# Sliding-window attention plus gated GLU on one Trainium2 core: the later chunks' normalised rows transposed through a DRAM scratch and VectorE, and a mask tile filled on another engine

## The chip, the cores and the metric

The kernel runs on 1 core of one Trainium2 chip. The metric is the device time of one execution in microseconds (us), the median of the runs of a kernel.

## The reference, cut to what matters

```python
xn = layernorm(x)                                  # x: 1 x 2048 x 640, no scale, no bias
qkv = xn @ wqkv                                    # 32 heads of 20
scores = q @ k.T * 20**-0.5                        # query i sees keys i-255 .. i
o = softmax(where(mask, scores, -1e9)) @ v
A = o @ wo
h = sigmoid(xn @ w_gate) * (xn @ w_up)             # 640 -> 1536
B = h @ w_down
out = x + A + B
```

All tensors are bf16. Every product of the normalised rows needs them with the 640 features on the partitions, because TensorE contracts over partitions. So the normalised x, whose rows have tokens on partitions, has to be transposed once. How this is done for three quarters of the tokens is what changes.

## The kernel before, in words

The 2048 tokens are cut into four chunks of 512 (`NCH`, `CW`), numbered 0 to 3. A chunk has four blocks of 128 tokens, called s = 0 to 3 (`SBC`), and the features make five blocks of 128, d = 0 to 4 (`DC`). For each chunk there are these stages:

- **norms.** `load_x` (L137) brings the chunk's rows to the tile `xc`, which has one buffer. `ln_block` (L261) takes means and variances on VectorE, one block at a time (two bn_stats at L252 and an aggregate at L258). `rstd_blocks` (L264) makes 1/sqrt(var+eps) on GpSimd. `norm_block` (L270, the operation is L272) writes the normalised rows to a tile `xn`. Then `xnT[c]`, the transposed chunk, is filled: for chunk 0 by TensorE (`transpose_rows`, L276), for chunks 1 to 3 by four DMA transposes from SP's queue (`turn_block`, L282, L283).
- **qk** (`g_qk`, L366): ten groups of five matmuls (L297) on `xnT`, copied out by VectorE (q, L301) or ScalarE (k, L303), stored to a DRAM scratch (L305) and loaded again spread by head (`spread`, L307, the DMA is L315).
- **v** (`g_v`, L385): eight groups of five matmuls (L326), copied out half by VectorE and half by ScalarE (both L335).
- **gu** (`g_gu`, L402): twelve pairs of a gate group (L411) and an up group (L418). ScalarE takes tanh of the gate (L414) and VectorE multiplies (`h`, L422).
- **scores, exp, mask, pv** (`scores`, L480; `pv`, L508): a step puts score matmuls (L487) into one PSUM tile, ScalarE takes the exponential into `pT` (L493), and GpSimd zeroes what the mask excludes (L504). In the last step of each group of a later chunk, VectorE does this instead with a minimum against the tile `edge` (L497). `pv` multiplies by v (L520). VectorE then transposes and scales the result (L532 to L548) into `oc`.
- **out** (`g_out`, L457): down projection (L432), output projection (L439), residual (`rows`, L443) and the store (L454).

TensorE's PSUM tiles of all stages but the scores come from one pool of four buffers, `ps_d`. A group of matmuls can start only when the reader of the tile that had its buffer is done.

The order of work on each engine is fixed by the program. The loop over score steps (L719) calls `fill.pull`, which takes pieces from a list of generators (L689 to L707), about 1800 ns of matmuls a step. `mix(a, b, first, every, rest)` (L595) runs generator `a` and, from its piece number `first` on, puts one step of `b` behind every `every`-th piece. So the norms of chunk 1 are threaded through the gu pieces of chunk 0, those of chunk 2 through `out0`, those of chunk 3 through `gu1b` and `out1`. Each engine then executes its own list in order: an instruction that waits holds up all that stands behind it on that engine, and SP's queue issues its DMAs in order as well.

`edge` (L236) is filled by GpSimd: a memset (L239) and four affine selects (L243). `make_edge` is called at L675, but GpSimd waits for nothing there and runs these instructions as soon as it reaches them.

Of the kernel before, what the change touches and what calls it, by code (L numbers as in the profile page):

```python
# [9 lines left out]
P = 128  # L10
S = 2048
D = 640
# [3 lines left out]
DC = D // P  # L16
FC = F // P
CW = 512
NCH = S // CW
SBC = CW // P  # L20
# [11 lines left out]
MULT = mybir.AluOpType.mult  # L32
SUB = mybir.AluOpType.subtract
# [3 lines left out]
BIG = 3.0e38  # L37
BF16 = mybir.dt.bfloat16
# [55 lines left out]
def kernel(  # L94
# [11 lines left out]
    nc = tc.nc  # L106
    x2 = A_x.flatten_outer_dims()
# [3 lines left out]
    def pool(name, bufs, **kw):  # L111
        return ctx.enter_context(tc.tile_pool(name=name, bufs=bufs, **kw))
# [3 lines left out]
    lnp = pool("lnp", 4)  # L116
# [18 lines left out]
    xc = {}  # L135

    def load_x(c):  # L137
        t = xp.tile([P, SBC, D], BF16, name="xc")
        xc[c] = t
        nc.sync.dma_start(out=t, in_=xr[:, c * SBC:(c + 1) * SBC, :])  # L140
# [39 lines left out]
    def load_gu(t, w, k, lo=0, hi=FS):  # L180
        nc.sync.dma_start(out=t[k][:, :, lo:hi],
                          in_=w.rearrange("(c p) f -> p c f", p=P)[:, :, k * FS + lo:k * FS + hi])
# [32 lines left out]
    def load_wo():  # L215
        for i in range(HG):
            nc.sync.dma_start(out=wo[32 * i:32 * i + 32, :, :],
                              in_=wo_i[i].rearrange("(m j) n -> j m n", j=32))
# [17 lines left out]
    edge = const.tile([P, HG, 2 * U], BF16, name="edge")  # L236

    def make_edge():
        nc.gpsimd.memset(edge, BIG)  # L239
        for k, base, sign in ((0, -1, -1), (1, 0, 1)):  # L240
            for a in range(2):
                view = edge[a * U:(a + 1) * U, :, k * U:(k + 1) * U]
                nc.gpsimd.affine_select(out=view, in_=view, pattern=[[0, HG], [sign, U]],  # L243
                                        compare_op=GE, fill=0.0, base=base, channel_multiplier=-sign)

    xnT = {}
    xns = {}
# [13 lines left out]
    def ln_block(c, s, mv=None):  # L261
        return ln_mv(ln_half(c, s, 1, ln_half(c, s, 0)), mv)

    def rstd_blocks(mvs):  # L264
        rstds = lnp.tile([P, SBC], FP32, name="rstds", bufs=1)
        nc.gpsimd.tensor_scalar(out=rstds, in0=mvs[:, :, 1], scalar1=EPS, scalar2=None, op0=ADD)
        nc.gpsimd.tensor_tensor(out=rstds, in0=rstds, in1=neghalf, op=POW)
        return rstds

    def norm_block(c, s, mv, rstd):  # L270
        xn = lnp.tile([P, D], BF16, name="xn")
        nc.vector.tensor_scalar(out=xn, in0=xc[c][:, s, :], scalar1=mv[:, 0:1],  # L272
                                scalar2=rstd[:, 0:1], op0=SUB, op1=MULT)
        xns[c, s] = xn
# [4 lines left out]
            nc.tensor.transpose(pt[:, d, :], xns[0, s][:, d * P:(d + 1) * P], ident)  # L279
        copy(out=xnT[0][:, lo:hi, s * P:(s + 1) * P], in_=pt[:, lo:hi, :])  # L280

    def turn_block(c, s):  # L282
        nc.sync.dma_start(out=xnT[c][:, :, s * P:(s + 1) * P], in_=xns.pop((c, s)), transpose=True)  # L283

    def new_xnT(c):
        xnT[c] = xtp.tile([P, DC, CW], BF16, name="xnT")
# [51 lines left out]
    def proj_v(c, s, hf, copy):  # L338
        copy_v(c, s, hf, project_v(c, s, hf), copy)

    MM = 216

    def g_norms(c, turn, gap=3):


        new_xnT(c)
        mvs = lnp.tile([P, SBC, nc.vector.BN_AGGR_DIM], FP32, name="mvs", bufs=1)
        for s in range(SBC):
            ln_block(c, s, mvs[:, s, :])
            if s == SBC - 1:  # L350
                rstds = rstd_blocks(mvs)
            yield 0
        for _ in range(gap):
            yield 0
        for s in range(SBC):
            norm_block(c, s, mvs[:, s, :], rstds[:, s:s + 1])
            yield 0
            if turn:
                turn_block(c, s)

    def g_turns(c):
        for s in range(SBC):
            turn_block(c, s)
            yield 0

    def g_qk(c):  # L366
        for w in "qk":
            for m in range(DC):
                proj_block(w, c, m)
                if c == 0 and w == "q" and m == 1:  # L370
                    load_x(1)
                if c == 0 and w == "q" and m == 3:
                    load_gu(wu, B_w_up, 0, FS // 2)
                if c == 1 and w == "q" and m == 3:
                    load_wo()
                if c and w == "k" and m == DC - 1:
                    spread("q", c, 0, GH)
                yield 5 * MM
        if c == 0:
            spread("q", c, 0, 2)  # L380
            spread("k", c, 0, 2)
            spread("q", c, 2, 4)
            spread("k", c, 2, 4)

    def g_v(c):  # L385
        for s in range(SBC):
            new_v(c, s)
            for hf in range(2):
                proj_v(c, s, hf, nc.scalar.copy if hf else nc.vector.tensor_copy)
                if hf == 0:  # L390
                    yield 5 * 136
            if s == 0:
                spread("k", c, 0, 2)
                spread("k", c, 2, GH)
            if s == 1:
                spread("q", c, GH, NG)
                spread("k", c, GH, NG)
            yield 5 * 136
# [4 lines left out]
    def part(w, d, f):  # L403
        k, first = divmod(f * P, FS)
        return w[k][:, d, first:first + P]

    def g_gu(c, f0, f1):
        for f in range(f0, f1):
            pg = ps_d.tile([P, CW], FP32, name="pg", tag="d")
            for d in range(DC):  # L410
                nc.tensor.matmul(pg, lhsT=part(wg, d, f), rhs=xnT[c][:, d, :],  # L411
                                 start=(d == 0), stop=(d == DC - 1))
            th = tp.tile([P, CW], FP32, name="th")
            nc.scalar.activation(out=th, in_=pg, func=TANH, scale=0.5)  # L414
            yield 5 * MM
            pu = ps_d.tile([P, CW], FP32, name="pu", tag="d")
            for d in range(DC):
                nc.tensor.matmul(pu, lhsT=part(wu, d, f), rhs=xnT[c][:, d, :],  # L418
                                 start=(d == 0), stop=(d == DC - 1))
            h = hp.tile([P, CW], BF16, name="h")  # L420
            ht[c, f] = h
            nc.vector.scalar_tensor_tensor(out=h, in0=th, scalar=1.0, in1=pu, op0=ADD, op1=MULT)  # L422
            yield 5 * MM
# [39 lines left out]
    def g_out(c, between, ahead=()):  # L463
        nxt = new_rows(c, 0)
        for s in range(SBC):
            rows = nxt
            if s == 0:
                yield from ahead
            if s + 1 < SBC:
                nxt = new_rows(c, s + 1)  # L470
            ys = [ps_d.tile([P, CW], FP32, name=f"y{i}", tag="d") for i in range(2)]
            for y, cut in zip(ys, HALVES):
                yield from down(c, s, y, cut)
            if s == 0:
                yield from between
            outp(c, s, ys, rows)
            yield 10 * 136
# [117 lines left out]
    def mix(a, b, first, every=1, rest=True):  # L595

        for k, cost in enumerate(a):
            yield cost
            if k >= first and (k - first) % every == 0:
                yield next(b, 0)  # L600
        if rest:
            yield from b
# [66 lines left out]
    nc.scalar.activation(out=scr, in_=neghalf[:, 0:1], func=EXP)  # L669
    banks.close()  # L670
    ps_s = banks.enter_context(tc.tile_pool(name="ps_s", bufs=1, space=bass.MemoryType.PSUM))
    for _ in g_qk(0):
        pass
    load_rest()
    make_edge()  # L675

    fill = Fill()
    GU = 10 * MM
    OUT = 4 * 34 * 136
    APART = 1800  # L680
    FIRST_PART = 1000
    def later(load, *args):
        load(*args)
        yield 0

    norms1 = g_norms(1, True)
    norms2 = g_norms(2, True)
    norms3 = g_norms(3, False, 6)
    fill.add("gu0a", mix(g_gu(0, 0, 4), norms1, 4, 1, False), 4 * GU)  # L689
    fill.add("gu0b", mix(g_gu(0, 4, 12), norms1, 0), 8 * GU)  # L690
    fill.add("x2", later(load_x, 2), 0)
    fill.add("wo_i", later(turn_wo), 0)
    fill.add("wd", later(load_wd), 0)
    fill.add("pads", later(clear_next), 0)
    fill.add("qk1", g_qk(1), 50 * MM)
    fill.add("v1", mix(g_v(1), g_gu(1, 0, 2), 1, 2), 40 * 136 + 2 * GU)
    fill.add("out0", mix(g_out(0, g_gu(1, 2, 3)), norms2, 1, 1), OUT + GU)
    fill.add("x3", later(load_x, 3), 0)
    fill.add("qk2", g_qk(2), 50 * MM)
    fill.add("v2", mix(g_v(2), g_gu(1, 3, 7), 0, 1), 40 * 136 + 4 * GU)  # L700
    fill.add("gu1b", mix(g_gu(1, 7, 12), norms3, 0, 1, False), 5 * GU)
    fill.add("out1", mix(g_out(1, g_gu(2, 0, 1)), itertools.chain(norms3, g_turns(3)), 1, 2), OUT + GU)
    fill.add("qk3", g_qk(3), 50 * MM)
    fill.add("v3", mix(g_v(3), g_gu(2, 1, 5), 0, 1), 40 * 136 + 4 * GU)
    fill.add("gu2", g_gu(2, 5, 12), 7 * GU)
# [38 lines left out]
    c = NCH - 1  # L744
# [6 lines left out]
    rows = [new_rows(c, s, *home, queue=nc.scalar) for s, home in enumerate(homes)]  # L751
# [55 lines left out]
```

## Time and profile before

| | before |
|---|---|
| runs, us | 309.04, 309.19, 309.59 (median 309.19) |
| span of the profiled execution, first to last instruction, us | 307.5 |
| TensorE busy (matmuls) | 299.6 us, 97% |
| VectorE, ScalarE, GpSimd busy | 170.7, 198.4, 169.3 us |
| DMA transposes | 12, from SP's queue |
| granted TensorE clock | 1.00 |

The profile's page gives the profiled execution by its span alone, which is 1.7 us below the median of the runs; what lies before the first and after the last instruction makes up the rest. A busy share is taken over the whole span. The lines below give times in us from the start of the span; "idle before" in square brackets is the time in which the engine stood still ahead of that piece, with what ended it.

### The profile page before, as it was taken

How to read it: one execution, taken by the hardware profiler on the slowest of the kernel's cores; microseconds unless marked ns; L12 is line 12 of the kernel's file. 1: busy time of each engine (PE TensorE's matmuls, PEld its weight loads, DVE VectorE, ACT ScalarE, POOL GpSimd, SP SyncE). 2: the span in 40 equal slices, each digit the busy share in tenths (PEclk: the TensorE clock that was granted, in tenths of full speed). 3: DMA queues.
4: the chain of work that ended last, by engine and by line, in shares of the span. 5: the costliest groups of instructions: out<-in, count | busy, mean ns of one | idle time of the engine just before them, and what ended most of it. 6: DMA issues, size and time to landing. Idle time of an engine off the chain costs nothing.

```text
span 307.5 us, 9944 instructions
## 1 busy us (share of the span) xinstructions
PE 299.6 (97%) x4276; PEld 167.5 (54%) x4311; DVE 170.7 (56%) x339; ACT 198.4 (65%) x197; POOL 169.3 (55%) x308
## 2 busy tenths in 40 slices
PE   7999999999999999999999999999999999999995
PEld 3654444555657654554457654554546664444774
DVE  5633666639698364487946164392824536363523
ACT  6933877698855649888674547878585547687000
POOL 6000686787874828576683729467372937566000
PEclk9999999999999999999999999999999999999999
DMA  7997976986407352820002712730000200000202
GB/s 215 366 344 236 324 158 214 337 238 209 154 2 139 58 179 68 272 83 2 3 3 67 129 58 87 250 122 0 5 0 2 87 26 21 2 2 7 83 21 67
DMA packets 40460, 35.68 MB, mean 116 GB/s; under 512 B 10560, under 2 KB 39872, under 8 KB 40384
## 3 DMA queue, kind: packets, MB, share of 16 engines
q1 hardware_dynamic: 39552, 34.27, 37.3%
q10 hardware_dynamic: 864, 0.77, 0.9%
q8 instruction: 34, 0.56, 0.8%
q14 instruction: 10, 0.08, 0.1%
HBM read 23.63 MB, written 10.26 MB: 110 GB/s over the span
## 4 chain that ended last, share of the span: by engine, by line
PE 96%; issue 1%; DMA 1%; DVE 1%; ACT 0%; SPq 0%
PE y L432 18%; PE pu L418 17%; PE pg L411 17%; PE pqk L297 14%; PE ps L487 9%; PE pv L326 7%; PE y L439 7%; PE acc L520 6%; DMA xc<-in_A_x_dram 1%; PE pt L279 0%; ACT xn L617 0%; DVE xn L272 0%; DVE xn L628 0%; SPq L156 0%; DVE stats L252 0%
## 5 line engine op out<-in xcount | busy, mean ns | idle before, releaser
L504 POOL TENSOR_SCALAR_AFFINE_SELECT pT<-pT 64x512 bf16<-64x512 bf16 (+1 forms) x256 | 157.7, 616 | 108.1 <-ACT pT L493 95.6
L493 ACT ACTIVATE pT<-ps 128x2048 bf16<-128x2048 f32 (+1 forms) x76 | 141.0, 1855 | 59.6 <-PE ps L487 54.6
L422 DVE SCALAR_TENSOR_TENSOR h<-th,pu 128x512 bf16<-128x512 f32 x48 | 32.8, 684 | 52.6 <-PE pu L418 46.1
L418 PE MATMUL pu<-xnT,wu 128*128 128x512 bf16 x228 | 59.0, 380 | 0.7 <-issue 0.2
L411 PE MATMUL pg<-xnT,wg 128*128 128x512 bf16 x226 | 58.5, 380 | 0.9 <-issue 0.3
L432 PE MATMUL y<-wd,h 128*128 128x320 bf16 (+2 forms) x396 | 56.7, 295 | 0.0
L432 PEld LDWEIGHTS <-h 128*128 128x128 bf16 x396 | 36.7, 98 | 15.8 <-issue 2.0
L414 ACT ACTIVATE th<-pg 128x512 f32<-128x512 f32 x48 | 28.6, 595 | 15.5 <-PE pg L411 15.4
L411 PEld LDWEIGHTS <-wg 128*128 128x128 bf16 x240 | 22.2, 98 | 25.8 <-issue 1.8
L418 PEld LDWEIGHTS <-wu 128*128 128x128 bf16 x240 | 22.0, 98 | 25.5 <-issue 2.0
L487 PE MATMUL ps<-qT,kT 20*64 20x320 bf16 (+4 forms) x1440 | 32.1, 260 | 0.0
L532 DVE STREAM_TRANSPOSE t<-acc 128x512 f32<-128x512 f32 x32 | 21.1, 697 | 19.7 <-PE acc L520 19.7
L487 PEld LDWEIGHTS <-kT 20*64 20x64 bf16 x1440 | 15.4, 103 | 24.9 <-issue 21.8
L443 DVE SCALAR_TENSOR_TENSOR rows<-y,rows 128x320 bf16<-128x320 f32 x30 | 14.4, 488 | 25.5 <-PE y L439 25.3
L544 DVE TENSOR_TENSOR on<-t,rec 128x320 bf16<-128x320 f32 (+4 forms) x48 | 27.8, 580 | 1.1
L326 PE MATMUL pv<-wv,xnT 128*128 128x320 bf16 x160 | 25.7, 300 | 0.0
L439 PE MATMUL y<-wo,oc 128*128 128x320 bf16 (+2 forms) x165 | 24.2, 295 | 0.0
L297 PE MATMUL pqk<-xnT,wk 128*128 128x512 bf16 x97 | 23.1, 381 | 0.2
L297 PE MATMUL pqk<-xnT,wq 128*128 128x512 bf16 x94 | 22.8, 381 | 0.4 <-issue 0.2
L335 DVE CAST v<-pv 64x320 bf16<-64x320 f32 x29 | 14.1, 486 | 12.5 <-PE pv L326 12.3
L520 PE MATMUL acc<-pT,v 64*32 64x320 bf16 (+4 forms) x1440 | 19.7, 253 | 0.0
L520 PEld LDWEIGHTS <-v 64*32 64x32 bf16 x1440 | 16.2, 91 | 5.8 <-ACT pT L493 1.7
(50 smaller groups left out, 178.7 us busy)
## 6 DMA issues: line engine op xcount, KB each, us to landing
qT<-sq SPq DMA_DIRECT2D x16, 256.0 KB
kT<-sk SPq DMA_DIRECT2D x16, 256.0 KB
sq<-st SPq DMA_DIRECT2D x20, 128.0 KB
sk<-st SPq DMA_DIRECT2D x20, 128.0 KB
out_dram<-rows SPq DMA_DIRECT2D x15, 160.0 KB
wg<-in_B_w_gate_dram SPq DMA_DIRECT2D x4, 480.0 KB
wu<-in_B_w_up_dram SPq DMA_DIRECT2D x4, 480.0 KB
xc<-in_A_x_dram SPq DMA_DIRECT2D x3, 640.0 KB
```

Source lines behind the costliest of these rows:

```text
L297: nc.tensor.matmul(ps, lhsT=wt[:, m, :], rhs=xnT[c][:, d, :], start=(d == 0), stop=(d == DC - 1))
L326: nc.tensor.matmul(ps[:, 0:HALF], lhsT=xnT[c][:, d, s * P:(s + 1) * P], rhs=wqkv[2][:, d, hf * HALF:(hf + 1) * HALF], start=(d == 0), stop ...
L411: nc.tensor.matmul(pg, lhsT=part(wg, d, f), rhs=xnT[c][:, d, :], start=(d == 0), stop=(d == DC - 1))
L414: nc.scalar.activation(out=th, in_=pg, func=TANH, scale=0.5)
L418: nc.tensor.matmul(pu, lhsT=part(wu, d, f), rhs=xnT[c][:, d, :], start=(d == 0), stop=(d == DC - 1))
L422: nc.vector.scalar_tensor_tensor(out=h, in0=th, scalar=1.0, in1=pu, op0=ADD, op1=MULT)
L432: nc.tensor.matmul(y[:, 0:cut[1] - cut[0]], lhsT=ht[c, f][:, s * P:(s + 1) * P], rhs=wd[:, f, cut[0]:cut[1]], start=(f == 0), stop=False)
L439: nc.tensor.matmul(y[:, 0:cut[1] - cut[0]], lhsT=oc[c, m][:, s * P:(s + 1) * P], rhs=wo[:, m, cut[0]:cut[1]], start=False, stop=(m == DC - 1))
L487: nc.tensor.matmul(ps[a * U:(a + 1) * U, i, col * U:(col + n) * U], lhsT=qk["k", kc, o // GH][32 * i:32 * i + DH, o % GH + a, kb * U:(kb + ...
L493: nc.scalar.activation(out=pt[:, :, 0:width], in_=ps[:, :, 0:width], func=EXP, scale=SCALE)
L504: nc.gpsimd.affine_select(out=view, in_=view, pattern=[[0, HG], [0, n], [sign, U]], compare_op=GE, fill=0.0, base=base, channel_multiplier ...
L520: nc.tensor.matmul(acc[32 * i:32 * i + 32, q * U:(q + n) * U], lhsT=vt[kb][a * U:(a + 1) * U, u, h * VW:h * VW + 32], rhs=pt[a * U:(a + 1) ...
```

## The change

For chunks 1 to 3 the DMA transposes go away. The normalised rows are written by VectorE with their features regrouped, stored by four DMAs of 160 KB to a scratch in DRAM (`xs`), and loaded back by four DMAs of 160 KB into the chunk's own `xc` tile, in runs of 320 bytes, so that partition 32b+j holds every 32nd token and the b-th quarter of the features. Five VectorE transposes of 32x32 blocks (`turn`), one for each d, then make `xnT[c]`. The steps of the norms generators are placed anew: `norms2` begins in `v1` and goes on in `out0`, the loads of x for chunks 2 and 3 move behind the first k store of the chunk before, and `lag` steps lie between the loads back and the first `turn`. Besides, `make_edge` moves ahead of the first qk stage and its memset goes to VectorE, while the selects stay on GpSimd.

```diff
-        nc.gpsimd.memset(edge, BIG)
+        nc.vector.memset(edge, BIG)
...
-    def turn_block(c, s):
-        nc.sync.dma_start(out=xnT[c][:, :, s * P:(s + 1) * P], in_=xns.pop((c, s)), transpose=True)
+    xs = [tc.dram_tile([CW, D], BF16, name=f"xs{k}") for k in range(2)]
+
+    def norm_grouped(c, s, mv, rstd):
+        xn = lnp.tile([P, D], BF16, name="xn")
+        nc.vector.tensor_scalar(out=xn.rearrange("p (b d i) -> p d b i", b=4, i=32),
+                                in0=xc[c][:, s, :].rearrange("p (d b i) -> p d b i", b=4, i=32),
+                                scalar1=mv[:, 0:1], scalar2=rstd[:, 0:1], op0=SUB, op1=MULT)
+        nc.sync.dma_start(out=xs[c % 2][s * P:(s + 1) * P, :], in_=xn)
+
+    def regroup(c):
+        rows = xs[c % 2].rearrange("(t j) (b f) -> b j t f", j=32, b=4)
+        for b in range(4):
+            nc.sync.dma_start(out=xc[c][32 * b:32 * b + 32].rearrange("j s (a f) -> j (s a) f", a=4), in_=rows[b])
+
+    def turn(c, d):
+        nc.vector.transpose(out=xnT[c][:, d, :].rearrange("p (t j) -> p t j", j=32),
+                            in_=xc[c].rearrange("p s (a f) -> p (s a) f", a=4)[:, :, 32 * d:32 * d + 32])
...
-    def g_norms(c, turn, gap=3):
-        new_xnT(c)
+    def g_norms(c, gap=3, lag=3):
...
         for s in range(SBC):
-            norm_block(c, s, mvs[:, s, :], rstds[:, s:s + 1])
+            norm_grouped(c, s, mvs[:, s, :], rstds[:, s:s + 1])
             yield 0
-            if turn:
-                turn_block(c, s)
-
-    def g_turns(c):
-        for s in range(SBC):
-            turn_block(c, s)
+        regroup(c)
+        for _ in range(lag):
+            yield 0
+        new_xnT(c)
+        for d in range(DC):
+            turn(c, d)
             yield 0
...
+                if c and w == "k" and m == 0 and c + 1 < NCH:
+                    load_x(c + 1)
...
+    make_edge()
     for _ in g_qk(0):
         pass
     load_rest()
-    make_edge()
...
-    norms1 = g_norms(1, True)
-    norms2 = g_norms(2, True)
-    norms3 = g_norms(3, False, 6)
-    fill.add("gu0a", mix(g_gu(0, 0, 4), norms1, 4, 1, False), 4 * GU)
+    norms1 = g_norms(1, 3, 7)
+    norms2 = g_norms(2)
+    norms3 = g_norms(3, 4, 4)
+    fill.add("gu0a", mix(g_gu(0, 0, 4), norms1, 1, 1, False), 4 * GU)
     fill.add("gu0b", mix(g_gu(0, 4, 12), norms1, 0), 8 * GU)
-    fill.add("x2", later(load_x, 2), 0)
...
-    fill.add("v1", mix(g_v(1), g_gu(1, 0, 2), 1, 2), 40 * 136 + 2 * GU)
+    fill.add("v1", mix(mix(g_v(1), g_gu(1, 0, 2), 1, 2), norms2, 3, 1, False), 40 * 136 + 2 * GU)
     fill.add("out0", mix(g_out(0, g_gu(1, 2, 3)), norms2, 1, 1), OUT + GU)
-    fill.add("x3", later(load_x, 3), 0)
...
-    fill.add("out1", mix(g_out(1, g_gu(2, 0, 1)), itertools.chain(norms3, g_turns(3)), 1, 2), OUT + GU)
+    fill.add("out1", mix(g_out(1, g_gu(2, 0, 1)), norms3, 1, 2), OUT + GU)
```

## The prediction

> **What bounds the kernel now.** I read the page's slices first (TensorE at 9 in 38 of 40), then TensorE's own waits, then the timelines of TensorE and VectorE around the places where the change works. TensorE's waits, in full but for the first row (columns: total us, times, longest):
>
> ```profile
> PE pt L279 <- DVE xn L272: 0.7, 1, 0.7
> PE pt L279 <- DVE xn L628: 0.5, 1, 0.5
> PE pg L411 <- issue: 0.3, 2, 0.2
> PE pqk L297 <- issue: 0.2, 1, 0.2
> PE pu L418 <- issue: 0.2, 1, 0.2
> ```
>
> After chunk 0's norms TensorE waits for nothing that has a name: matmuls follow each other from 13 us to 303 us. So there is little to win (at most the 1.2 us of the first two rows), and every new wait of TensorE is lost time. In particular no transpose of `xnT` by DMA is waited for: by the landing counts in the trace they land at 46.7, 102.7 and about 175.3 us, and qk starts at 54.6, 107.3 and 178.3 us.
>
> **The start.** GpSimd's selects of `edge` ran from 3.9 to 5.7 us. VectorE's norm at 4.81 us, beside them, took 0.64 us, the later ones at 7.61 and 9.60 us 0.45 us each. The change takes the selects away: at most 0.2 us, and the next transposes hang on ScalarE's root, which ends at 5.72 us either way. I take -0.1 (0 to -0.2). The memset on VectorE (0.69 us on GpSimd) fits into its 0.66 us pause before 14.18 us, and may cost 0.1 there.
>
> **Chunk 1.** The rows store behind the third norm at about 39.6 us, land at 43 (behind q and k transfers that land until 41.5), and the loads back, issued from 43 to 45, land near 47.6. The first `turn` stands behind the tenth `h`, at 51.1 us: that wait is covered by 3.5 us. The last turn stands behind the twelfth `h`:
>
> ```profile
> 53.06 1.24 PE L418 MATMUL pu<-xnT,wu 128*128 128x512 bf16 x5
> 54.59 2.35 PE L297 MATMUL pqk<-xnT,wq 128*128 128x512 bf16 x10
> ...
> 51.79 0.69 DVE L422 SCALAR_TENSOR_TENSOR h<-th,pu 128x512 bf16<-128x512 f32 x1 [0.59 <-PE pu L418]
> 54.57 0.69 DVE L422 SCALAR_TENSOR_TENSOR h<-th,pu 128x512 bf16<-128x512 f32 x1 [2.09 <-ACT th L414]
> ```
>
> A turn is not in the trace. Its nearest row is the transpose of `oc` (128x512 bf16, 0.71 us, next instruction 0.64 us after its start); I take that, although the turn reads in pieces of 64 bytes, and keep 0.4 to 1.0 us. The last h starts at 54.57 (ScalarE's tanh holds it), the fifth turn ends at about 55.95, and the fifth matmul of qk is due at 54.6 + 4 x 0.213 = 55.5: **+0.45** (0 to 1.9, the latter with turns of 1.0 us).
>
> **Chunk 2, in v of chunk 1.** Here the statistics, 4.0 us of VectorE (the eight bn_stats and four aggregates that ran from 86.81 to 90.79), move forward between the copies of v:
>
> ```profile
> 74.35 0.99 DVE L335 CAST v<-pv 64x320 bf16<-64x320 f32 x2
> 75.37 0.69 DVE L422 SCALAR_TENSOR_TENSOR h<-th,pu 128x512 bf16<-128x512 f32 x1
> 76.31 0.99 DVE L335 CAST v<-pv 64x320 bf16<-64x320 f32 x2 [0.25 <-PE pv L326]
> 79.21 0.99 DVE L335 CAST v<-pv 64x320 bf16<-64x320 f32 x2 [1.91 <-PE pv L326]
> 81.04 0.69 DVE L422 SCALAR_TENSOR_TENSOR h<-th,pu 128x512 bf16<-128x512 f32 x1 [0.83 <-PE pu L418]
> 81.92 1.31 DVE L532 STREAM_TRANSPOSE t<-acc 128x512 f32<-128x512 f32 x2 [0.19 <-PE acc L520]
> ```
>
> On the clock of before, counted from the end of the first row (75.3): two blocks of statistics to 77.3, h to 77.9, a third to 78.9, the third copy to 79.75, the fourth block to 80.75, the last copy to 81.7 instead of 80.2. By the changed program's waits, the second accumulator of the next `pv` takes the buffer that this last copy frees; it is due at about 80.95. So TensorE waits **+0.8** (0 to 1.5; pauses of 3 us shown above take up most of the 4). The x rows must have landed by 75.3; issued near 66, behind transfers that then land 4 us late, they do by about 71.5. They also lie ahead of four k stores. Scores need those k at 77.96, before they landed at 76.2; what is moved forward costs their 1.8 us of packets, but the same transfer no longer lies ahead at 45: I take nothing, 0 to 1.
>
> **Chunk 2, the round trip.** From 81.7 on VectorE has no pause: the first norm waits for GpSimd's roots (1.3 us behind the last statistics, 82.35), then norm, h, two transposes of acc, norm, the chain of scaling (3.7 us, as from 83.16 to 86.88 before), and two norms: 0.55 each, as in the rows of 0.41 to 0.75 us of the norms before. The last norm ends at about **90.15**. Only then can its store be issued. A store of 160 KB issued at 92.26 landed at 94.03, so this one lands at 91.95. The four loads wait for all four stores; a load of 160 KB took 2.3 us from issue to landing, three more issues follow at 0.45 us or three more transfers at 0.75 us: the last lands at about **96.5**. But VectorE comes to the first turn at 91.75, behind the residual of out0's first block. It stands still for 4.7 us, and behind the turns stands this:
>
> ```profile
> 91.35 0.88 DVE L443 SCALAR_TENSOR_TENSOR rows<-y,rows 128x320 bf16<-128x320 f32 x2
> 94.21 0.43 DVE L497 TENSOR_TENSOR pT<-pT,edge 128x512 bf16<-128x512 bf16 x1 [0.27 <-ACT pT L493]
> 95.06 0.87 DVE L443 SCALAR_TENSOR_TENSOR rows<-y,rows 128x320 bf16<-128x320 f32 x2
> ...
> 95.17 1.29 PE L520 MATMUL acc<-pT,v 64*32 64x320 bf16 x96
> 96.39 0.43 PE L487 MATMUL ps<-qT,kT 20*64 20x320 bf16 x24
> 96.75 2.62 PE L432 MATMUL y<-wd,h 128*128 128x320 bf16 x18
> ```
>
> Four turns bring it to 99.05, the minimum (0.43) to 99.5. The `pv` of before 95.17, shifted by the 0.8 to 95.97, needs the minimum's result two thirds through, at 96.75: it waits 2.8 us. After it, the down projection (96.75 in the last row) needs the buffer of the residual that follows the fifth turn: another 0.25. Together **+3.05**. Bounds: 1.0 (norms of 0.41, all loads in parallel, landing at 94.6) and 5.5 (norms of 0.75, turns of 1.0, transfers of 1.2 us each).
>
> **Chunk 3.** Its round trip has 8 us, from about 161 to the first turn at 169. The last turn stands behind the last residual of out1 (178.07 + 0.49), ends near 179.2, and the fifth matmul of qk is due at 179.2: **+0.1** (0 to 0.6). Where TensorE is late, ScalarE and GpSimd only gain slack, and SP's queue is left by 12 DMA transposes of 1.2 us issue each for 24 issues of 0.45.
>
> **The sum:** -0.1 + 0.45 + 0.8 + 3.05 + 0.1 = +4.3 us, on the span of 307.5: 311.8. The 1.7 us outside the span stay, so 309.19 becomes 313.5.
>
> **The rivals.** *Hidden round trip:* the rows are there when VectorE comes to chunk 2's first turn, and it never stands still. Price: the 3.05 go, and the total is 310.4; 309.6 if pauses absorb v's wait too, 309.2 without chunk 1's term, and 308.1 if the start's whole 1.2 us are won besides. It decides at one point: the last norm would have to end by about 85.4 instead of 90.15. For it speaks that my VectorE clock adds 25 durations in a row; against it that the list of VectorE puts two norms behind the scaling chain, which needs a `pv` that ends at 81.9. Chance 0.14.
>
> *Slow short runs:* the loads back write 2048 runs of 320 bytes. Packets of 384 bytes took 22 ns in the trace, of 640 bytes 32, of 1024 bytes 46: a line through these gives 20 ns, 2.6 us for all on 16 engines, which is inside the forecast. If a run under some length cost double, 2.6 us are added ahead of chunk 2's turns: 316.1; chunk 1 still has 3.5 of cover. The 256-byte packets of the DMA transposes at 18 ns speak against it. Chance 0.10. The Trainium skill, in "DMA: Bandwidth & Descriptors", section Specifications, puts the least run for full rate at 512 bytes, with a read-modify-write below; by that rule the time would be this rival's, and no row here shows a plain load of such runs.
>
> *Other causes,* mostly slower (a k transfer late for 77.96, turns that hold GpSimd): 0.06.
>
> The Trainium skill, in "VectorE: DVE Perf Modes", section The three transpose paths, calls VectorE's transpose the quickest for 32x32 blocks, 311 ns against 1309 ns by DMA for 128x128. It says nothing about the time, as the DMA's transposes held up nobody here.
>
> **How the numbers follow.** The forecast has 0.70, its own range 311.0 to 316.2 (each term's low or high end, not all at once). To hold 8 in 10 the range reaches down to 310.2 and up to 317.0, which takes in the slow runs and the upper part of the hidden case. About 0.2% (0.6 us) is what can be told from no change. Of the hidden case I count 0.07 as faster, 0.05 as the same and 0.02 as slower, of the other causes 0.01 each as faster and the same: 0.08, 0.06 and, with the rest, 0.86 slower.
>
> **What would show it.** Right: VectorE's waits list a new row, the turn waiting for a DMA of `xc` from `xs`, 4 to 5 us once, near 92 to 97 us; TensorE waits for the minimum (L512 after) about 2.8 us near 97, for VectorE's copy of v some 0.8 us near 81, and under a microsecond before qk of chunk 1. Wrong: TensorE's waits stay as above, or the stall sits in front of a qk stage or of chunk 1's first scores.

## The result, and the profile after

| | before | after |
|---|---|---|
| runs, us | median 309.12 (308.95 to 309.59, 4 runs) | median 317.63 (315.91 to 320.22, 4 runs) |
| ratio after to before | | 1.0281, 95% interval 1.0233 to 1.0329 |
| profiled execution, us | span 307.5 | 317.51, span 315.1 |
| TensorE, VectorE busy, us | 299.6, 170.7 | 305.6, 178.5 |

The prediction said 313.5 (310.2 to 317.0). The direction holds; the loss is about twice as large. The line numbers of the kernel after: norm L286, store to the scratch L289, loads back L295, turn L298, qk L313, pv of the v stage L342, v copy L351, h L437, down L447, output projection L454, residual L458, exp L508, minimum L512, `acc` L535, `t` L547, `oc` L563.

In the page's slices of the kernel after, the row of the granted TensorE clock is no longer 9 all along, as it was before:

```profile
PE   7999999999895999999999999999999999999996
PEclk9999999999998799999999999999999999999999
```

Each digit is 7.9 us. TensorE loses in slice 11 (about 79 to 87 us) and in slice 13 (about 95 to 102 us), and the clock is down in slices 13 and 14. TensorE's waits after (engine, line, what was waited for, total us, times, longest) name two new places of weight, and one small one:

```profile
PE acc L535 <- DVE pT L512: 3.3, 1, 3.3
PE acc L535 <- DVE v L351: 0.9, 1, 0.9
...
PE pqk L313 <- DVE xnT L298: 0.3, 1, 0.3
```

They are the three waits that the prediction put on the path, in its places. VectorE's waits have the row that it asked for, too:

```profile
DVE xnT L298 <- DMA xc<-xs: 5.9, 1, 5.9
```

To see what each costs, I take the start of the same score step in both traces and subtract. The score steps run through the whole kernel, so the difference shows where time is lost, and that it is lost there for good (us, times of before, shift of the other kernels against before; the labels are those of the experiments below):

| score step at, before | after | e1_busy | lag5 | e3_early | e5_delay11 | e6_late_turns | e7_delay8 | e8_stats | e9_moved | e10_pauses | e11_long | e13_behind |
|---|---|---|---|---|---|---|---|---|---|---|---|---|
| 54.23 | +0.08 | +0.03 | +0.05 | +0.04 | +0.09 | +0.23 | +1.77 | +0.08 | +0.04 | +0.05 | +0.25 | +0.28 |
| 77.96 | +0.52 | +0.47 | +0.49 | +0.52 | +0.09 | +0.67 | +1.77 | +0.31 | +0.04 | +0.05 | +0.71 | +0.30 |
| 91.72 | +1.69 | +1.64 | +1.66 | +5.35 | -0.01 | +1.84 | +1.67 | +1.48 | -0.06 | +0.77 | +1.88 | +0.20 |
| 101.94 | +8.00 | +5.72 | +5.94 | +5.35 | +4.23 | +1.84 | +3.16 | +1.48 | -0.06 | +0.77 | +6.90 | +0.20 |
| 113.49 | +8.00 | +5.72 | +5.94 | +5.35 | +4.23 | +1.84 | +3.16 | +1.48 | +4.47 | +0.77 | +6.90 | +0.20 |
| 281.40 | +8.02 | +6.70 | +5.94 | +5.35 | +4.22 | +1.86 | +3.18 | +1.51 | +4.49 | +0.78 | +6.91 | +0.23 |

For the kernel after the steps are 0.08 at the start, 0.44 in chunk 1, 1.17 in v of chunk 1, 6.31 between 91.72 and 101.94, and nothing from there to the end: chunk 3's round trip is hidden. (The medians differ by 8.5 us; the trace is of one execution, the second fastest of the four.)

Why 6.31, where TensorE waits 3.34? TensorE's timeline around the place:

```profile
96.86 0.91 PE L535 MATMUL acc<-pT,v 64*32 64x320 bf16 x64
101.11 0.95 PE L535 MATMUL acc<-pT,v 64*32 64x256 bf16 x32 [3.34 <-DVE pT L512]
101.99 0.65 PE L502 MATMUL ps<-qT,kT 20*64 20x320 bf16 x24
102.57 4.79 PE L447 MATMUL y<-wd,h 128*128 128x320 bf16 x18
```

The 18 matmuls of the down projection, in the last row, took 2.62 us before and take 4.79 us here, with nothing waited for in between. The busy times by stretch (us, PE, PEld, DVE, ACT, POOL, then the granted clock, DMA share, GB/s) give the reason:

```profile
98.00:100.00 2.00, 0.00 (x0) 0.00 (x0) 1.74 (x3) 0.00 (x0) 0.00 (x0) 1.00 0.01 4
...
102.00:104.00 2.00, 2.00 (x38) 1.24 (x31) 1.97 (x6) 1.20 (x1) 0.00 (x0) 0.50 0.30 88
104.00:106.00 2.00, 2.00 (x9) 1.09 (x8) 1.93 (x5) 0.68 (x1) 1.20 (x2) 0.50 0.29 79
...
108.00:110.00 2.00, 2.00 (x23) 1.28 (x29) 0.49 (x1) 1.72 (x1) 0.21 (x1) 1.00 0.00 0
```

The granted clock stands at 0.50. By the clock's records in the trace it does so from 100.21 to 107.04 us. TensorE works from 101.11, so 5.93 us run at half speed, which costs 2.97; with the wait of 3.34 that is the 6.31.

VectorE's rows there show the wait as the prediction told it. The stand-still is 5.9 us, since the last load lands at 98.1 by the landing counts:

```profile
91.89 0.49 DVE L458 SCALAR_TENSOR_TENSOR rows<-y,rows 128x320 bf16<-128x320 f32 x1 [0.19 <-PE y L454]
98.26 2.49 DVE L298 STREAM_TRANSPOSE xnT<-xc 128x512 bf16<-128x512 bf16 x4 [5.88 <-DMA xc<-xs]
100.67 0.38 DVE L512 TENSOR_TENSOR pT<-pT,edge 128x512 bf16<-128x512 bf16 x1
```

### The profile page after: what moved, and what is told of

It is laid out like the page before. It is cut to its first block, busy times and chain, and to the rows that moved or that the text cites. A ratio compares the mean times of both kernels' runs of the same rounds, so it can differ in the third digit from the quotient of the medians.

```text
span 315.1 us, 10002 instructions
## 1 busy us (share of the span) xinstructions
PE 305.6 (97%) x4311; PEld 169.2 (54%) x4311; DVE 178.5 (57%) x355; ACT 198.5 (63%) x197; POOL 168.8 (54%) x307
## 4 chain that ended last, share of the span: by engine, by line
PE 86%; DVE 7%; DMA 3%; issue 2%; ACT 1%; SPq 1%; POOL 0%; DVEq 0%; ACTq 0%
PE y L447 16%; PE pu L433 16%; PE pg L426 16%; PE pqk L313 14%; PE ps L502 8%; PE y L454 6%; PE acc L535 5%; PE pv L342 5%; DMA xc<-xs 1%; DVE on L559 1%; DVE stats L252 1%; DVE xnT L298 1%; DVE v L351 1%; DMA xc<-in_A_x_dram 1%; DVE oc L563 1%
## 5 line engine op out<-in xcount | busy, mean ns | idle before, releaser
L508 ACT ACTIVATE pT<-ps 128x2048 bf16<-128x2048 f32 (+1 forms) x76 | 141.0, 1855 | 67.5 <-PE ps L502 64.1
L437 DVE SCALAR_TENSOR_TENSOR h<-th,pu 128x512 bf16<-128x512 f32 x48 | 32.7, 681 | 49.3 <-PE pu L433 43.4
L433 PE MATMUL pu<-xnT,wu 128*128 128x512 bf16 x240 | 59.8, 380 | 0.0
L426 PE MATMUL pg<-xnT,wg 128*128 128x512 bf16 x240 | 59.8, 380 | 0.0
L447 PE MATMUL y<-wd,h 128*128 128x320 bf16 (+2 forms) x396 | 58.8, 303 | 0.0
L447 PEld LDWEIGHTS <-h 128*128 128x128 bf16 x396 | 37.6, 100 | 16.9 <-issue 1.8
L547 DVE STREAM_TRANSPOSE t<-acc 128x512 f32<-128x512 f32 x32 | 21.1, 695 | 19.4 <-PE acc L535 19.4
L458 DVE SCALAR_TENSOR_TENSOR rows<-y,rows 128x320 bf16<-128x320 f32 x30 | 14.5, 487 | 26.6 <-PE y L454 26.5
L559 DVE TENSOR_TENSOR on<-t,rec 128x320 bf16<-128x320 f32 (+4 forms) x48 | 26.8, 557 | 1.1
L342 PE MATMUL pv<-wv,xnT 128*128 128x320 bf16 x160 | 25.6, 300 | 0.1
L535 PE MATMUL acc<-pT,v 64*32 64x320 bf16 (+4 forms) x1440 | 20.5, 255 | 4.2 <-DVE pT L512 3.3
L454 PE MATMUL y<-wo,oc 128*128 128x320 bf16 (+2 forms) x165 | 24.2, 295 | 0.0
L313 PE MATMUL pqk<-xnT,wq 128*128 128x512 bf16 x100 | 23.5, 381 | 0.3 <-DVE xnT L298 0.3
L313 PE MATMUL pqk<-xnT,wk 128*128 128x512 bf16 x100 | 23.2, 381 | 0.0
L535 PEld LDWEIGHTS <-v 64*32 64x32 bf16 x1440 | 16.6, 92 | 10.4 <-issue 6.8
L351 DVE CAST v<-pv 64x320 bf16<-64x320 f32 x29 | 14.1, 485 | 10.4 <-PE pv L342 10.1
```

The source lines that it names most:

```text
L313: nc.tensor.matmul(ps, lhsT=wt[:, m, :], rhs=xnT[c][:, d, :], start=(d == 0), stop=(d == DC - 1))
L342: nc.tensor.matmul(ps[:, 0:HALF], lhsT=xnT[c][:, d, s * P:(s + 1) * P], rhs=wqkv[2][:, d, hf * HALF:(hf + 1) * HALF], start=(d == 0), stop ...
L447: nc.tensor.matmul(y[:, 0:cut[1] - cut[0]], lhsT=ht[c, f][:, s * P:(s + 1) * P], rhs=wd[:, f, cut[0]:cut[1]], start=(f == 0), stop=False)
L454: nc.tensor.matmul(y[:, 0:cut[1] - cut[0]], lhsT=oc[c, m][:, s * P:(s + 1) * P], rhs=wo[:, m, cut[0]:cut[1]], start=False, stop=(m == DC - 1))
L508: nc.scalar.activation(out=pt[:, :, 0:width], in_=ps[:, :, 0:width], func=EXP, scale=SCALE)
L535: nc.tensor.matmul(acc[32 * i:32 * i + 32, q * U:(q + n) * U], lhsT=vt[kb][a * U:(a + 1) * U, u, h * VW:h * VW + 32], rhs=pt[a * U:(a + 1) ...
```

## The experiments

Theory T1: the wait of TensorE for the minimum brings the granted clock down, and that costs 3 us beyond the wait. Rival R1: those 3 us are a backlog of VectorE and of PSUM buffers behind the turns, and the clock goes along with it.

### The halved clock

**e1_busy** keeps TensorE working in the wait and leaves all else.

```diff
 in pv, ahead of the pieces that wait for the minimum of chunk 1's first group
...
+            if (c, o, k) == (1, 0, 8):
+                spare = ps_s.tile([P, HG, CW], FP32, name="spare", tag="ps")
+                for r in range(14):
+                    nc.tensor.matmul(spare[:, r % HG, :], lhsT=ones[:, 0:P], rhs=ones, start=True, stop=True)
```

> The kernel after, with 14 extra matmuls of 512 columns into a spare score buffer (about 3.0 us of TensorE at 0.213 us each; the result is used by nothing) placed just ahead of the pv pieces that wait 3.34 us for the minimum on VectorE. VectorE's work is unchanged, so the minimum comes at the same time. Theory T1 (the granted TensorE clock halved for 6.8 us because TensorE stood idle for 3.34 us, and this cost 3.0 us): TensorE stays busy, the clock stays at 1.0 through 100 to 107 us, and the time falls by 2.5 to 3.5 us below the kernel after, to about 314.5, although work was added. Rival R1 (the 3.0 us come from buffers and VectorE work backed up behind the four turns, and the clock does nothing): the time stays at 317.5 or rises.

Measured: 315.60 us (314.72 to 316.38), ratio to before 1.021 (1.0188 to 1.0231). TensorE's wait and the same stretch as above:

```profile
PE acc L539 <- DVE pT L512: 0.6, 1, 0.6
```

```profile
102.00:104.00 2.00, 1.94 (x44) 1.47 (x37) 2.00 (x6) 1.38 (x1) 0.00 (x0) 1.00 0.19 57
```

The clock stays at 1.00 to the end of the work (the mean of each of the four runs is 0.999 or 1.000), and the kernel gets faster by adding work: the shift behind the place is 5.72 instead of 8.00, and the median is 2.0 us lower, a little less than the 2.5 to 3.5 expected. Of the 2.97, 0.37 are given back because the spare matmuls took 3.23 us and the last pieces of `pv` began that much later than in the kernel after; about as much again has no cause that the trace names. Near 210 us this execution lost 0.96 us more, in one gap of 0.89 us for which the profile names no engine ("issue"); no other trace has it, and I can't say what it was. R1 is wrong: the same turns stood on VectorE, and it waited for the loads as long (6.2 us).

**e5_delay11 and e7_delay8** make the wait in the kernel before, with nothing of the change: memsets on VectorE ahead of the same minimum.

```diff
+    idle = const.tile([P, HG, 2 * U], BF16, name="idle")
...
+            if (c, o) == (1, 0):
+                for _ in range(11):        # e7_delay8: range(8)
+                    nc.vector.memset(idle, 0.0)
             late()
```

> The kernel before, with none of the change, but with eleven memsets of a 128x512 bf16 tile on VectorE (an estimate of 0.3 to 0.5 us each, 3.5 to 5 us) ahead of the same minimum in chunk 1's first group. Nothing is loaded, stored or turned in addition. TensorE must then wait some 2.5 to 4 us for the minimum. T1: the granted clock halves behind that wait and the time rises by the wait plus about 3 us, 5.5 to 7 in all. R1 (the loss belongs to the turns and the buffers behind them): the time rises by the wait alone, 2.5 to 4 us, and the clock stays at 1.0.

> The kernel before, with eight instead of eleven memsets ahead of the same minimum. By 4.19 us for eleven, three fewer are 1.14 us less, so TensorE waits 2.48 - 1.14 = 1.3 us. T1 with a wait that is long enough to bring the clock down lying between 0.9 us (the wait for the copy of v, which did not) and 2.3 us (lag of five, which did): the clock stays at 1.0 and the time rises by 1.3 us to 310.4. If 1.3 us are enough: by 1.3 + 1.7 = 3.0 us to 312.1.

Measured: e5_delay11 312.72 us (311.80 to 313.51), ratio 1.0116 (1.0089 to 1.0144); e7_delay8 310.52 (310.36 to 312.33, 10 runs), ratio 1.0045 (1.0022 to 1.0068). The long wait as TensorE's timeline and the stretches have it:

```profile
98.55 0.71 PE L522 MATMUL acc<-pT,v 64*32 64x256 bf16 x32 [2.48 <-DVE pT L499]
99.18 0.65 PE L489 MATMUL ps<-qT,kT 20*64 20x320 bf16 x24
99.77 3.83 PE L434 MATMUL y<-wd,h 128*128 128x320 bf16 x18
```

```profile
100.00:102.00 2.00, 2.00 (x9) 1.18 (x8) 1.97 (x6) 1.88 (x1) 0.06 (x1) 0.50 1.31 149
```

A wait of 2.48 us moved all that follows by 4.24: the clock is halved from 98.86 to 102.27 us, 3.41 us, which costs 1.71 (2.48 + 1.71 = 4.19). The total came out below the 5.5 to 7 expected, since the clock was down for at most one such stretch and not for two. The four runs show the same in pairs: 313.39 (the profiled one) and 313.51 us have mean granted clocks of 0.993 and 0.994, while 311.80 and 312.04 us have 0.999 and 0.998. One program, with the same wait written into it, is 1.5 us slower where the clock went down; and a wait of this length does not bring it down every time. With eight memsets TensorE waited 1.3 us, the clock stayed up, and the wait cost 1.5. (That execution also began with 1.7 us lost, since its clock rose only at 10.2 us, in the other traces at 3.5 to 6.7 us. The median of its runs doesn't contain that.)

**lag5** shortens the wait in the kernel after, by two turns fewer ahead of the minimum.

```diff
-    norms2 = g_norms(2)
+    norms2 = g_norms(2, 3, 5)
```

> The kernel after, with five steps instead of three between the loads back of chunk 2 and its first turn, so that two turns fewer stand ahead of the minimum on VectorE. The wait of TensorE in chunk 2 shortens from 3.34 to about 2.1 us (two turns of 0.62 us less); the turns themselves are only moved. T1: if 2.1 us are too short for the clock to fall, it stays at 1.0 and the time falls by 1.2 + 3.0 = 4.2 us to about 313.3; if it falls all the same, by 1.2 to about 316.3. R1 (backlog of VectorE): by 1.2 at most, since as many turns as before stand ahead of qk of chunk 2, and the clock's record does not change the time.

Measured: 314.99 us (314.46 to 315.61), ratio 1.0192 (1.0175 to 1.0208). TensorE waited 2.33 us, and the clock was halved from 101.85 to 105.27, 3.41 us. The time fell by 2.6 us (medians), more than R1's 1.2 and less than T1's 4.2: 1.0 less wait, and one stretch of halved clock instead of two. The clock fell in all four runs (means of 0.993 to 0.995).

**e3_early** was meant to shorten the round trip by earlier norms.

```diff
-    norms2 = g_norms(2)
+    norms2 = g_norms(2, 1, 5)
```

> The kernel after, with the norms of chunk 2 two steps earlier and the first turn two steps later against the loads back (gap 1 and lag 5 instead of 3 and 3), so the turns stand where they stood, and the rows are stored some 1 to 3 us earlier. T1: VectorE's stand-still before the turns shrinks from 5.9 us to 3 to 5, TensorE's wait from 3.34 to 0.5 to 2.3, and if the clock then stays at 1.0 the time falls by 4 to 6 us, to 311.5 to 313.5. R1: by the shortening alone, 1 to 3 us, to 314.5 to 316.5. If the norms, now ahead of the scaling chain, delay that chain instead, a new wait of TensorE appears for it and part is given back.

Measured: 315.44 us (314.20 to 317.29), ratio 1.0225 (1.0193 to 1.0258). The number lies in R1's range, but not by R1's mechanism, and T1's numbers failed. The round trip was hidden (VectorE did not wait for the loads), but the first norm now stood ahead of the last copy of v, and waited 1.48 us there for GpSimd's roots:

```profile
PE acc L535 <- DVE v L351: 3.0, 1, 3.0
```

The clock fell for 3.41 us again, at 85.46, though no turn ran near. So it does not take the turns or the minimum. This execution, 314.20 us, is the fastest of the four; the others have mean clocks of 0.985 to 0.988 against its 0.995, so there it was down for longer.

### The other terms

**e8_stats** is the kernel before, its DMA transposes kept, with the load of x and the statistics of chunk 2 moved into v of chunk 1.

```diff
+                if (c, w, m) == (1, "k", 0):
+                    load_x(2)
...
-    fill.add("x2", later(load_x, 2), 0)
...
-    fill.add("v1", mix(g_v(1), g_gu(1, 0, 2), 1, 2), 40 * 136 + 2 * GU)
+    fill.add("v1", mix(mix(g_v(1), g_gu(1, 0, 2), 1, 2), norms2, 3, 1, False), 40 * 136 + 2 * GU)
```

> The kernel before with its DMA transposes, but with the load of x for chunk 2 and the statistics and norms of chunk 2 begun in v of chunk 1, as in the kernel after. Theory: the 1.17 us that TensorE loses there come from the 4 us of statistics among the copies of v, so the time rises by 1.2 us to about 310.3, with a wait of the first accumulator matmuls for the last copy of v of 0.9 us near 81 us. Rival: they come from something else of the change (the store and loads of the scratch, the turns of chunk 1): the time stays at 309.1.

Measured: 310.42 us (310.01 to 310.58, 10 runs), ratio 1.003 (1.0013 to 1.0048), and a shift of 1.17 at that place, to the hundredth that of the kernel after. So the 1.17 belong to the order of VectorE's work, not to the scratch.

**e11_long** asks what the short runs of the loads back cost.

```diff
-        rows = xs[c % 2].rearrange("(t j) (b f) -> b j t f", j=32, b=4)
+        rows = xs[c % 2].rearrange("(s b j) f -> b j s f", b=4, j=32)
...
-            nc.sync.dma_start(out=xc[c][32 * b:32 * b + 32].rearrange("j s (a f) -> j (s a) f", a=4), in_=rows[b])
+            nc.sync.dma_start(out=xc[c][32 * b:32 * b + 32], in_=rows[b])
```

> The kernel after, with the four loads back reading the same 160 KB each to the same 32 partitions in runs of 1280 instead of 320 bytes (the tokens then lie in another order, so this kernel computes something else from chunk 1 on; the amount of work is the same). Rival of the prediction (short runs cost double, 2.6 us for the four): the last load lands 2.6 us earlier, near 95.3, VectorE stands still 3.3 instead of 5.9 us, TensorE waits 0.7 instead of 3.3, the clock stays at 1.0, and the time falls by 5.6 us to 312. If the length of the runs costs nothing: 0.8 to 0.9 us a load as before, and 317.5. In between, the share that run length has in the stand-still can be read from the landing.

Measured: 316.19 us (314.94 to 316.81), ratio 1.021 (1.0179 to 1.0241).

```profile
DVE xnT L298 <- DMA xc<-xs: 5.5, 1, 5.5
```

From the first load's issue to the last landing it is 4.90 us, against 5.71 with runs of 320 bytes: a share of 0.8 us, not 2.6. (TensorE's wait is 3.0 instead of 3.3 us, and the clock was down for one stretch instead of two.) The packets of 320 bytes took 20 ns each in the trace of the kernel after, as the prediction's line had them. The rival of the slow short runs is refuted. The Trainium skill's rule of 512 bytes ("DMA: Bandwidth & Descriptors", section Specifications) made far less difference here than a doubling.

**e12_edge** is the kernel before with the edge part alone.

```diff
-        nc.gpsimd.memset(edge, BIG)
+        nc.vector.memset(edge, BIG)
...
+    make_edge()
     for _ in g_qk(0):
         pass
     load_rest()
-    make_edge()
```

> The kernel before with the edge part of the change alone: the memset on VectorE, and all of it called ahead of qk of chunk 0. The prediction gave the start -0.1 us; the kernel after shows +0.08 at the first score. Theory: no time either way, 309.1 to 309.3; TensorE's two waits at the start hang on ScalarE's root and not on the norm that the selects slowed. Rival (the selects cost the start up to 0.2 us): 308.9 to 309.0.

Measured: 309.01 us (308.69 to 310.69, 12 runs), ratio 0.9988 (0.9969 to 1.0006). No difference that can be told from none; the numbers of theory and rival lie too close together to be told apart.

### The change placed elsewhere

**e6_late_turns** puts all five turns of chunk 2 behind the minimum.

```diff
-    norms2 = g_norms(2)
+    norms2 = g_norms(2, 3, 8)
```

> The kernel after, with eight steps instead of three between the loads back of chunk 2 and its first turn: all five turns stand behind the minimum and behind the transposes of the next two accumulators. The change is whole; only its turns of chunk 2 are placed otherwise. T1: neither the wait of TensorE for the minimum nor the halved clock is left, and of the 8.0 us remain 0.1 at the start, 0.44 in chunk 1 and 1.17 in v of chunk 1, 1.7 us in all: about 310.9. A rival by which the loads back themselves, or the turns wherever they stand, cost TensorE time: 313 or more, with a new wait ahead of qk of chunk 2.

Measured: 310.93 us (310.57 to 311.68, 10 runs), ratio 1.0042 (1.0023 to 1.0062); no wait for the minimum, clock 1.00. The same round trip, with its loads back and turns, costs nothing once nothing urgent stands behind it: 6.3 of the 8.0 us go with one number.

**e9_moved, e10_pauses, e13_behind** take away the other two terms as well. All have `norms1 = g_norms(1, 2, 7)`, which puts the last turn of chunk 1 ahead of the twelfth h.

```diff
 e9_moved
-    norms2 = g_norms(2)
+    norms2 = g_norms(2, 0, 7)
-    fill.add("v1", mix(mix(g_v(1), g_gu(1, 0, 2), 1, 2), norms2, 3, 1, False), 40 * 136 + 2 * GU)
+    fill.add("v1", mix(g_v(1), g_gu(1, 0, 2), 1, 2), 40 * 136 + 2 * GU)
 e10_pauses, against the kernel after
+    norms2 = g_norms(2, 0, 9)
+    fill.add("v1", mix(mix(g_v(1), g_gu(1, 0, 2), 1, 2), norms2, 7, 1, False), 40 * 136 + 2 * GU)
 e13_behind, against e10_pauses
-    norms2 = g_norms(2, 0, 9)
+    norms2 = g_norms(2, 1, 8)
```

> The kernel after with three steps placed anew: the norms of chunk 1 one step earlier (gap 2), so that its last turn stands ahead of the twelfth h; the statistics of chunk 2 back in out0, where the kernel before has them; and a lag of seven there, so that the five turns stand behind the residual of the third block, in the 4.4 us in which VectorE waits for TensorE in the kernel before (102.5 to 106.9). Theory (all of the loss is placement): the terms of chunk 1 (0.44), of v (1.17) and of the round trip (6.3 with the clock) all go, and the time is 309.1 to 309.6. Rival (the round trip through DRAM costs TensorE time wherever it is placed): 310.5 or more, with a wait ahead of qk of chunk 2 for a turn.

Measured: 311.29 us (308.88 to 314.09, 10 runs), ratio 1.0028 (0.9991 to 1.0064). The terms of chunk 1, of v and of the minimum are gone (shift -0.06 at 101.93), but now the round trip ends too late for qk of chunk 2. In the profiled execution the loads landed near 107.8, and TensorE waited for the turns:

```profile
PE pqk L313 <- DVE xnT L298: 2.1, 5, 1.2
```

The clock fell there too, from 111.61 to 115.02. Three of the ten runs came in at 309.21 or less, so here the landing is on the edge. The profiled run, 313.29, and the slowest have a mean clock of 0.995; the five in between, 310.7 to 311.8, have 0.998 and more. For this placement the rival's number and its wait ahead of qk came true.

> The kernel after, with chunk 1's norms one step earlier, and chunk 2's steps placed by the pauses that VectorE has in the kernel before: the four statistics behind the third copy of v in v1 (two in the pause of 1.9 us, two behind the last copy), all five turns behind the scaling of the next group. Against the version with the statistics in out0, whose loads back landed at 107.9 us and held up qk of chunk 2, the norms end 5 us earlier, near 91. Theory (all of the loss is placement): no named wait of TensorE is left, the clock stays at 1.0, and the time is 309.0 to 309.5 in every run, the same as the kernel before. Rival (the change costs TensorE something wherever it is placed): 310 or more.

Measured: 310.06 us (309.67 to 311.13, 12 runs), ratio 1.0028 (1.0013 to 1.0043). That is above the theory's 309.0 to 309.5. One wait is left, of the kind that e3_early showed, because the first norm waited for the roots ahead of the scaling of `oc`:

```profile
PE y L454 <- DVE oc L563: 0.6, 1, 0.6
```

> The version with the statistics in VectorE's pauses, with one step more between statistics and norms: the first norm, which stood still 1.16 us for GpSimd's roots and ran 0.6 us ahead of the scaling of the last pv of chunk 0, moves behind that scaling, with the other three. There the output projection waited 0.65 us for the second oc, the only wait of TensorE that the version had and the kernel before has not. Theory (all of the loss is placement): the second oc ends 1.7 us earlier, near 88.2 us, that wait goes, the clock stays at 1.0, and the time is that of the kernel before, 309.0 to 309.4. Rival (the change costs TensorE something wherever it is placed): a new wait takes its place, and the time stays at 309.8 to 310.1.

Measured: 309.21 us (308.77 to 310.81, 11 runs), ratio 1.0009 (0.9997 to 1.0020) against 309.12 of the kernel before. TensorE's waits in full but for the first row, which is at 0.8 us ahead of its first matmul:

```profile
PE pt L279 <- DVE xn L643: 0.6, 1, 0.6
PE pg L426 <- issue: 0.3, 2, 0.2
PE pv L342 <- DMA wv<-in_A_wqkv_dram: 0.2, 1, 0.2
PE pqk L313 <- issue: 0.2, 1, 0.2
PE pu L433 <- issue: 0.2, 1, 0.2
```

No wait that the change brought is left (the row of `wv` lies at 7 us, in the start). One of the eleven runs, 310.81, has a mean clock of 0.994, the others 0.998 and more: one stretch of halved clock would give that, and no trace shows where. So the change, placed like this, wins nothing and costs nothing that can be told from none (the interval ends at 0.2%); the 8 us were its placement. None of these kernels is faster than the kernel before by more than can be told apart.

## Why the prediction was right and wrong, point by point

| term | predicted | measured |
|---|---|---|
| start | -0.1 | +0.08 |
| chunk 1, last turn | +0.45 | +0.44 |
| chunk 2, statistics in v | +0.8 | +1.17 |
| chunk 2, wait for the minimum | +2.8 | 3.34 |
| chunk 2, wait for the buffer behind it | +0.25 | none seen |
| chunk 2, the halved clock | not foreseen | 2.97 |
| chunk 3 | +0.1 | 0.0 |

**The step that failed** is the last one of the round trip: "it waits 2.8 us", and from there straight into the sum. A wait of TensorE was priced at its own length. The runs show that a wait of this length can cost more: 4.24 us for 2.48 in the profiled execution of e5_delay11, without any of the change, and 2.28 us won back in e1_busy by filling it. In the kernel after the halved clock cost 2.97 us, most of the 3.7 by which the shift of 8.0 exceeds the forecast 4.3. The granted clock was noted as 1.00 ahead of the prediction, but the prediction itself does not name it, and none of its cases had a fall of it. The range (up to 317.0) took in the upper ends of the waits, and so did not reach 317.6.

**The mechanism of chunk 2 was right**, in every link: the stores could not go before the last norm (measured end 90.6, predicted 90.15), VectorE stood still for the loads (5.9, predicted 4.7), four turns and the minimum followed, and TensorE waited two thirds into that `pv`. The loads were mis-sized most: 5.71 us from first issue to last landing, predicted 4.55; e11_long gives 0.8 of the 5.71 to the short runs. The turn was sized well: four took 2.49 us, 0.62 each, predicted 0.64.

**v of chunk 1** was right in place and low in size: the last copy of v ended at 82.54, where the prediction's 81.7, moved by the 0.52 of shift ahead of it, gives 82.2; a wait of 0.9 shows, and 1.17 of shift. **The start** gained nothing: VectorE's first norm took 0.45 instead of 0.64 us, and TensorE waited 0.3 instead of 0.7 us for it, but then 0.7 instead of 0.5 us for the second norm, which hangs on ScalarE's root; and the clock rose at 4.64 instead of 4.24 us. The kernels that share this start are 0.03 to 0.28 us late at 54.23, so +0.08 is not a size of its own. **The hidden round trip** (rival, 0.14) did not come in this kernel, but e6_late_turns and e13_behind show that it exists, with the turns placed behind the minimum. The point that the rival had named, an earlier norm, hid it too (e3_early), but the earlier norm brought a new wait of 3.0 us.

What stays open: the runs of the kernel after spread over 4.3 us (those of before over 0.6). By their spans and mean granted clocks (0.988 to 0.993) the clock took an estimated 2.2 us of the fastest, 315.91, and 3.5 to 3.8 of the others. That explains the fastest, but not the slowest: 320.22 is 2.6 us above the median with only 0.3 more lost to the clock, and it has no trace.

## What to carry to other kernels

Where TensorE never idles, price a new wait of it at its length and, if it is like those here that brought the clock down, besides at half of the stretch for which the clock is then halved. Here the single waits that did so were 2.3 us and longer, one of 1.3 us did not, and one stretch was 3.4 us, so up to 1.7 us more; where there were two, they cost 3.0. The fall is not certain: two of the four runs of e5_delay11 show none. When a transfer is put into an engine's order, look at what stands behind the instruction that waits for it: moving the waiting instruction behind the urgent one was worth 6.3 us, moving the norms ahead of it earlier brought new waits (e3_early, e10_pauses). Steps that are moved forward belong into pauses that the timeline shows, and not between two instructions that another engine waits for.

## What the runs showed of the hardware

The granted clock has two values in these traces, 1.0 and 0.5, and every stretch at 0.5 inside the work lasted 3.41 us, or 6.83, twice that, in the kernel after. The stretches at 1.0 between the first rise and the fall last multiples of 3.41 as well (95.57 is 28 times, 92.16 is 27 times, 81.92 is 24 times). So the clock seems to be decided on a grid of 3.41 us. Worked out on that grid, the windows inside the work that end in a fall held 1.4 (e9_moved, in five gaps of 1.23 us and less) to 2.7 us (e3_early) of idle TensorE; the 1.3 us of e7_delay8 and the waits of 0.9 us did not bring it down. But idle time on this grid does not settle it: the first window of e3_early, to 6.96 us, held 1.6 us and was followed by no fall, and in e12_edge the last matmul ended 1.8 us before the end of a window, at 305.79, and the clock fell only at 309.20, one window later.

The Trainium skill, "TensorE: Matmul & The Clock Gate", section Part 1: The HAM clock gate, describes such a gate, with a free-running window of 3413 ns that agrees with the 3.41 here, and lets the clock fall after at least one idle window of about 3.4 us. The measurement differs in that: one wait of 2.33 us (lag5) and one of 2.48 (e5_delay11) were enough in the profiled executions, and by the mean clocks lag5 had a fall in each of its four runs and e5_delay11 in two of four. So the window need not be idle as a whole. How busy a window must be, and why the same wait brings the clock down in one run and not in the next, can't be told from these runs. That it hangs on where the wait falls on the grid would fit, but only one execution of each kernel has a trace.
